# RWKV-6 attention and a SwiGLU block in one kernel: eps kept in a column of x, PSUM tiles that name their rings, and another written order

## The chip, the cores and the metric

One core of a Trainium2 chip runs the whole program. The metric is the device time of one execution in microseconds, the median of several runs.

## The reference

Two layers. The first is a linear-attention recurrence over 768 positions for 4 batches and 8 heads of 48 channels; the second normalises its output and puts it through a gated feed-forward block.

```python
state = np.zeros((B, H, D, D))                       # B, H, S, D = 4, 8, 768, 48
for t in range(S):
    cur = einsum('bhd,bhe->bhde', u * k[t], v[t])
    y[t] = einsum('bhd,bhde->bhe', r[t], state + cur)
    state = w[t][..., None] * state + einsum('bhd,bhe->bhde', k[t], v[t])
x = y.transpose(0, 2, 1, 3).reshape(B * S, H * D)    # 3072 x 384
xn = x / sqrt(mean(x * x) + 1e-6) * rms_g
g = xn @ w_gate                                      # 384 x 1536
out = (g * sigmoid(g) * (xn @ w_val)) @ w_out        # 1536 x 384
```

## The kernel before, in words

The sequence is cut into six blocks of 128 positions, numbered n from 0 to 5; j is the batch (0 to 3) and a block of all four batches has 512 tokens. Blocks 0 and 1 are loaded together (256 positions, one load for each of r, k, v, w and each batch) and handled as a pair. Within a block the recurrence is written as matmuls. `ln` takes the logarithm of w (ACT), `cs_mm` and `cs_k` sum it along the positions (PE), `exp_r` and `exp_k` turn the sums into decay factors (ACT), `r_mul` (DVE) and `k_mul` (POOL, some on DVE) apply them to r and k. `rk_pe` transposes the result on PE for blocks 0 and 1, with `rk_tr` as the copy out of PSUM; for later blocks `rk_tr` is a transposing DMA. `q_mm` makes the scores, `q_mask_e` (DVE) masks the even heads, `q_copy_o` copies the odd heads out (ACT, or masked on DVE where `ODD_DVE` says so), and `q_mask_o` (POOL) masks them where ACT only copied. The diagonal term goes over `bonus_mul` (two POOL instructions), `bonus_sum` (DVE) and `bonus_v` (POOL). `cast_v` puts v into bf16, `st_mm` and `st_new` carry the state on, `y_mm` makes the output of the attention.

Then comes the norm: `x_add` (DVE) adds the diagonal term, `x_sq` squares and sums (ACT), `x_rstd` takes the power -1/2 (two POOL instructions, or ACT), `xn_mul` scales, `xn_pe` and `xn_out` transpose and apply the gain (blocks 4 and 5: a transposing DMA, `xn_tr`, and `xn_gain`). In the feed-forward part a block has 12 units `gate_mm`, `silu`, `val_mm`, `h_mul` of six 256-column matmuls in block 0 and three 512-column matmuls later, and then one `o_mm`, `o_out`, `out_dma` for each batch; the last batch of block 5 is cut into three of these (j = 3, 4, 5: 192, 96 and 96 columns).

Block 0's gates and vals begin once `xn_out.0.0` and `xn_out.1.0` are done. Their weights come in two groups, units 0 to 3 and 4 to 11, by `load_gv.g.h` (g the group; h = 0 for gate, 1 for val), and `w_out` in three by `load_wo`; these loads convert to bf16 and are issued by POOL, in its queue. All other loads and the stores are issued by SP.

The order of the work is written out by hand: the string `ORDER` lists steps `function.n.j`, the program emits them in that order, and each engine carries out its own instructions in the order in which they were emitted. `warm` is a matmul on zeros whose result nobody reads.

PSUM has eight banks in three rings, a (2), b (2) and q (4). `psum` gives a step the bank whose last reader stands furthest back. Gates use a, vals b, everything small q, cumulative sums a and b.

```python
slots = rings[ring]
k = min((x for x in range(len(slots)) if slots[x][0] < at[0]), key=lambda x: slots[x])
...
slots[k] = [last_use.get(key, -1), taken[0]]
return psP.tile(shape, dtype, name="ps_" + ring + "uvxz"[k])
```

In the profile a bank is named by ring and letter: `ps_au`, `ps_bv`, `ps_qz`. Line 646 holds the matmuls of gates and vals, 683 those of o_mm, 238 all ACT functions with a table, 248 and 258 the loads of r, k, v, w, 350 and 353 the loads of weights, 464 and 465 bonus_mul, 457 k_mul, 475 bonus_v, 536 q_mask_o, 589 and 590 x_rstd on POOL.

## Time and profile before

| What | Value |
|---|---|
| Time, median of 3 runs | 199.3 us (199.29 to 199.4) |
| Span of the profiled execution | 197.6 us (its own device time is not listed; the runs' median is 1.7 us above this span) |
| PE (matmul) busy | 191.5 us, 97%, 1742 matmuls |
| PE weight loads busy | 120.4 us, 61% |
| DVE | 156.4 us, 79%, 315 instructions |
| ACT | 139.1 us, 70%, 286 |
| POOL | 127.5 us, 64%, 181 |
| Granted TensorE clock | 1.0 throughout |
| DMA | 32.42 MB, 155 GB/s of HBM traffic over the span |

A busy share is time in which the engine carried out something. PE's matmuls overlap each other in the records, so its share alone does not say that it had no slack; the waits and the chain do. A row of the timeline gives start, duration, engine, line, operation, output and inputs, and in brackets how long the engine had been idle and what ended that. "To landing" of a DMA counts from its issue.

### The profile page before, as it was taken

How to read it: one execution, taken by the hardware profiler on the slowest of the kernel's cores; microseconds unless marked ns; L12 is line 12 of the kernel's file. 1: busy time of each engine (PE TensorE's matmuls, PEld its weight loads, DVE VectorE, ACT ScalarE, POOL GpSimd, SP SyncE). 2: the span in 40 equal slices, each digit the busy share in tenths (PEclk: the TensorE clock that was granted, in tenths of full speed). 3: DMA queues.
4: the chain of work that ended last, by engine and by line, in shares of the span. 5: the costliest groups of instructions: out<-in, count | busy, mean ns of one | idle time of the engine just before them, and what ended most of it. 6: DMA issues, size and time to landing. Idle time of an engine off the chain costs nothing.

```text
span 197.6 us, 4751 instructions
## 1 busy us (share of the span) xinstructions
PE 191.5 (97%) x1742; PEld 120.4 (61%) x1742; DVE 156.4 (79%) x315; ACT 139.1 (70%) x286; POOL 127.5 (64%) x181
## 2 busy tenths in 40 slices
...
GB/s 164 320 325 267 244 220 205 220 213 197 174 230 162 199 179 214 200 211 214 185 206 225 202 147 166 227 51 145 134 216 12 5 60 60 20 63 80 40 60 101
DMA packets 109807, 32.42 MB, mean 164 GB/s; under 512 B 104276, under 2 KB 108632, under 8 KB 109784
## 3 DMA queue, kind: packets, MB, share of 16 engines
...
q10 hardware_dynamic: 8, 0.00, 0.0%
HBM read 25.96 MB, written 4.72 MB: 155 GB/s over the span
## 4 chain that ended last, share of the span: by engine, by line
PE 83%; DMA 7%; POOL 6%; SPq 1%; issue 1%; ACT 0%; POOLq 0%
PE ps_bu L646 13%; PE ps_bv L646 12%; PE ps_av L646 11%; PE ps_au L646 11%; PE ps_qv L683 7%; PE ps_qx L683 6%; PE ps_qz L683 6%; DMA wv_sb<-in_moe_w_val_dram 5%; PE ps_qu L683 5%; DMA kt<-in_k_dram 2%; POOL ruk L464 1%; POOL ruk L465 1%; SPq L248 1%; POOL qts L536 1%; PE ps_qz L513 1%
## 5 line engine op out<-in xcount | busy, mean ns | idle before, releaser
L238 ACT ACTIVATE sg<-ps_av 128x512 bf16<-128x512 f32 x36 | 21.5, 596 | 27.1 <-PE ps_av L646 21.4
L683 PEld LDWEIGHTS <-ht 128*128 128x128 bf16 x312 | 28.6, 98 | 18.3 <-DVE ht L666 0.4
L646 PEld LDWEIGHTS <-wg_sb 128*128 128x128 bf16 x252 | 27.0, 114 | 16.6 <-issue 0.3
L646 PEld LDWEIGHTS <-wv_sb 128*128 128x128 bf16 x252 | 26.4, 114 | 16.0 <-DMA wv_sb<-in_moe_w_val_dram 0.7
L666 DVE TENSOR_TENSOR ht<-ps_bu,sg 128x512 bf16<-128x512 f32 x37 | 25.4, 687 | 10.7 <-PE ps_bu L646 8.3
L666 DVE TENSOR_TENSOR ht<-ps_bv,sg 128x512 bf16<-128x512 f32 x35 | 24.0, 686 | 9.9 <-PE ps_bv L646 8.5
L646 PE MATMUL ps_bu<-xnt,wv_sb 128*128 128x512 bf16 (+1 forms) x135 | 30.3, 343 | 0.5 <-DMA wv_sb<-in_moe_w_val_dram 0.5
L646 PE MATMUL ps_av<-xnt,wg_sb 128*128 128x512 bf16 (+1 forms) x126 | 29.4, 350 | 0.0
L646 PE MATMUL ps_au<-xnt,wg_sb 128*128 128x512 bf16 (+1 forms) x126 | 29.3, 349 | 0.1
L646 PE MATMUL ps_bv<-xnt,wv_sb 128*128 128x512 bf16 (+1 forms) x117 | 28.5, 358 | 0.0
L464 POOL TENSOR_TENSOR ruk<-rt,kt 128x384 f32<-128x384 f32 x24 | 24.0, 1002 | 1.9 <-DVE diag L469 1.4
L465 POOL TENSOR_TENSOR ruk<-ruk,u_bc 128x384 f32<-128x384 f32 x24 | 24.0, 1000 | 1.9
L238 ACT ACTIVATE sg<-ps_au 128x512 bf16<-128x512 f32 x36 | 21.5, 596 | 4.5 <-PE ps_au L646 3.3
L457 POOL TENSOR_TENSOR rk<-kt,ek 128x384 bf16<-128x384 f32 x20 | 19.8, 1001 | 6.6 <-DMA kt<-in_k_dram 5.5
L475 POOL TENSOR_TENSOR ydiag<-vt,diag 128x384 f32<-128x384 f32 x24 | 19.9, 836 | 1.0 <-DVE diag L469 1.0
L236 ACT ACT_TABLE_LOAD x14 | 18.0, 1283 | 1.9 <-PEq L729 1.6
L536 POOL TENSOR_SCALAR_AFFINE_SELECT qts<-qts 128x512 bf16<-128x512 bf16 x19 | 11.9, 637 | 11.2 <-ACT qts L533 8.0
L683 PE MATMUL ps_qv<-wo_sb,ht 128*128 128x384 bf16 (+1 forms) x96 | 15.5, 311 | 0.0
L581 ACT ACTIVATE junk<-xb 128x384 bf16<-128x384 f32 x24 | 12.5, 521 | 4.2 <-DVE xb L576 3.9
L469 DVE TENSOR_REDUCE diag<-ruk 128x8 f32<-128x384 f32 x24 | 13.0, 544 | 0.0
L683 PE MATMUL ps_qx<-wo_sb,ht 128*128 128x384 bf16 x72 | 12.7, 326 | 0.0
L683 PE MATMUL ps_qz<-wo_sb,ht 128*128 128x384 bf16 x72 | 12.7, 326 | 0.0
(212 smaller groups left out, 376.8 us busy)
## 6 DMA issues: line engine op xcount, KB each, us to landing
...
wt<-in_w_dram SPq DMA_DIRECT2D x4, 384.0 KB, 4.3
rt<-in_r_dram SPq DMA_DIRECT2D x4, 384.0 KB, 4.9
kt<-in_k_dram SPq DMA_DIRECT2D x4, 384.0 KB, 4.9
```

Of the source, the lines that this page charges most:

```text
L236: nc.scalar.preload_act_table_set(table_name)
L238: return nc.scalar.activation(**kw).ins
L457: eng.tensor_tensor(out=rk[:, n % 2, j, 1, :, 0:D], in0=inp["k", n, j], in1=bank["cs_k", n, j][:, 0:DM].rearrange("p (h d) -> p h d", h=H) ...
L464: eng.tensor_tensor(out=ruk[n, j], in0=inp["r", n, j], in1=inp["k", n, j], op=ALU.mult)
L465: eng.tensor_tensor(out=ruk[n, j], in0=ruk[n, j], in1=u_bc, op=ALU.mult)
L469: nc.vector.tensor_reduce(out=diag[n, j].rearrange("p h o -> p (h o)"), in_=ruk[n, j], axis=mybir.AxisListType.X, op=ALU.add)
L475: eng.tensor_tensor(out=ydiag[n, j], in0=inp["v", n, j], in1=diag[n, j].to_broadcast([128, H, D]), op=ALU.mult)
L536: nc.gpsimd.affine_select(out=qts[n, j][:, 1], in_=qts[n, j][:, 1], compare_op=ALU.is_ge if n < 2 and j // 4 < n else ALU.is_gt, fill=0.0, ...
L581: nc.scalar.activation(out=junk, in_=xb[n, j], func=AF.Square, accum_out=rstd[n, j][:, 0:1])
L646: nc.tensor.matmul(ps.rearrange("p (i t) -> p i t", t=cols.stop - cols.start)[:, i, :], lhsT=units(ws, c, fs.start + i), rhs=xnt[n][:, c, ...
L666: nc.vector.tensor_tensor(out=ht[n][:, fs, cols], in0=bank.pop(("v", n, f)).rearrange("p (i t) -> p i t", i=fs.stop - fs.start), in1=bank. ...
L683: nc.tensor.matmul(ps[:, cols], lhsT=ht[n][:, f, b * L:(b + 1) * L], rhs=wo_sb[:, f, cols], start=(f == 0), stop=(f == FC - 1))
```

## The change

Four things, all in one edit.

- `ORDER` is another order of nearly the same steps. Steps for `warm` go from 34 to 41, those for `q_mask_o` from 19 to 18; all other steps are the same ones in other places.
- The sets that choose an engine for a step change: which `cast_v`, `xn_mul`, `rk_tr`, `q_copy_o`, `x_rstd`, `o_out` run on ACT, DVE or POOL. By count, DVE gets five more xn_mul and one more q_copy_o, and gives up one rk_tr and four o_out (two of them of part width) to ACT; POOL gets two more casts and gives up one mask.
- `MOVED_Q`, `MOVED_A`, `MOVED_B` name PSUM tiles that take their bank from another ring than their function's.
- x lives in four slots of one tile `xrow`, each with a 385th column that holds sqrt(eps x 384), set once. `x_sq` squares 385 columns with a scale of 384^-1/2, so its sum is already mean + eps; `x_rstd` needs one POOL instruction instead of two, and no `eps_col`.

```diff
 ORDER = """
 warm.200.0 warm.201.0 ... warm.209.0
-warm.210.0 warm.211.0 warm.212.0 load_w.0.0 load_w.0.1 ln.0.0 ln.0.1 load_r.0.0 load_k.0.0 cs_k.0.0 exp_k.1.0
-k_mul.1.0 cs_mm.0.0 exp_k.0.0 gu_mm.0.0 load_r.0.1 gu_out.0.0 load_k.0.1 exp_r.0.0 k_mul.0.0 bonus_mul.0.0 exp_r.1.0
-cs_mm.0.1 cs_k.0.1 exp_r.0.1 load_w.0.2 exp_k.0.1 r_mul.0.0 r_mul.1.0 load_w.0.3 r_mul.0.1 bonus_mul.0.1 bonus_mul.1.0
-exp_k.1.1 load_k.0.2 rk_pe.0.0 rk_tr.0.0 k_mul.1.1 rk_pe.1.0 warm.13.2 warm.14.2 warm.15.2 load_v.0.0 k_mul.0.1
-rk_tr.1.0 bonus_sum.0.0 w_tot.0.0 load_gv.1.0 exp_r.1.1 load_r.0.2 q_mm.0.0 warm.16.0 q_mm.1.4 warm.17.1 warm.18.2
-q_mask_e.0.0 r_mul.1.1 ln.0.2 ln.0.3 q_copy_o.0.0 cs_k.0.2 q_copy_o.1.4 exp_k.1.2 cs_mm.0.2 w_tot.0.1 q_mask_e.1.4
-bonus_v.0.0 load_v.0.1 q_mask_o.1.4 exp_k.0.2 q_mm.1.0 rk_pe.1.1 warm.19.1 warm.20.1 warm.21.2 q_copy_o.1.0
-bonus_sum.0.1 q_mask_e.1.0 exp_r.0.2 k_mul.1.2 cast_v.0.0 q_mm.0.4 warm.22.0 load_r.0.3 bonus_sum.1.0 load_k.0.3
-exp_r.1.2 q_copy_o.0.4 cast_v.1.0 rk_pe.0.1 rk_tr.0.1 q_mask_o.1.0 cs_mm.0.3 q_mask_e.0.4 rk_tr.1.1 r_mul.1.2
-bonus_v.1.0 exp_k.0.3 exp_r.0.3 y_mm.0.0 warm.23.0 q_mm.0.5 warm.24.0 warm.25.2 x_add.0.0 q_copy_o.0.5 y_mm.1.0
-q_mask_o.0.5 cast_v.1.1 q_mask_e.0.5 cast_v.0.1 load_v.0.2 r_mul.0.2 x_sq.0.0 x_add.1.0 rk_pe.1.2 load_w.2.0
-load_w.2.1 rk_tr.1.2 q_mm.0.1 warm.26.0 warm.27.0 warm.28.0 warm.29.2 q_copy_o.0.1 q_mask_e.0.1 exp_r.1.3 load_gv.1.1
-q_mm.1.1 warm.30.2 x_rstd.0.0 st_mm.0.0 k_mul.0.2 w_tot.0.2 x_sq.1.0 q_mask_e.1.1 xn_mul.0.0 load_v.0.3 bonus_v.0.1
-x_rstd.1.0 y_mm.0.1 rk_pe.0.2 q_copy_o.1.1 load_w.2.3 w_tot.0.3 xn_pe.0.0 st_new.0.0 xn_mul.1.0 x_add.0.1 cs_k.0.3
-rk_tr.0.2 exp_k.1.3 xn_out.0.0 x_sq.0.1 bonus_mul.1.1 r_mul.0.3 xn_pe.1.0 warm.31.1 warm.32.2 xn_out.1.0 q_mm.1.5
-warm.33.1 gate_mm.0.2 silu.0.2 gate_mm.0.3 silu.0.3 q_mask_o.1.1 q_mask_e.1.5 x_rstd.0.1 bonus_sum.1.1 q_copy_o.1.5
-q_mm.1.2 r_mul.1.3 load_r.2.0 k_mul.1.3 bonus_v.1.1 bonus_mul.0.3 y_mm.1.1 xn_mul.0.1 x_add.1.1 gate_mm.0.5
-gate_mm.0.4 q_mm.1.6 q_mask_e.1.2 load_gv.0.0 k_mul.0.3 q_copy_o.1.2 q_mask_e.1.6 silu.0.5 load_gv.0.1 bonus_mul.1.2
-rk_pe.1.3 rk_tr.1.3 val_mm.0.3 xn_pe.0.1 xn_out.0.1 h_mul.0.3 q_copy_o.1.6 x_sq.1.1 val_mm.0.5 x_rstd.1.1 q_mm.1.7
...
-gate_mm.0.1 cast_v.0.3 load_wo.1.0 x_sq.1.2 q_mask_o.0.6 silu.0.0 bonus_v.0.2 y_mm.0.2 q_mm.1.3 q_mask_e.1.3 silu.0.1
...
-out_dma.4.2 out_dma.4.3 silu.5.6 h_mul.5.6 o_mm.4.1 h_mul.5.5 silu.5.9 o_out.4.1 val_mm.5.10 out_dma.4.1 val_mm.5.9
-h_mul.5.9 gate_mm.5.10 silu.5.10 h_mul.5.10 o_mm.5.2 o_mm.5.3 o_out.5.2 o_out.5.3 o_mm.5.0 out_dma.5.2 o_out.5.0
-o_mm.5.1 out_dma.5.3 o_out.5.1 o_mm.5.4 out_dma.5.0 out_dma.5.1 o_mm.5.5 o_out.5.4 out_dma.5.4 o_out.5.5 out_dma.5.5
+warm.210.0 warm.211.0 warm.212.0 load_w.0.1 ln.0.1 cs_mm.0.1 load_w.0.0 ln.0.0 exp_r.0.1 w_tot.0.1 warm.0.1 cs_mm.0.0
+exp_k.0.0 exp_r.1.0 gu_mm.0.0 gu_out.0.0 load_r.0.0 load_k.0.0 r_mul.1.0 load_r.0.1 r_mul.0.1 load_k.0.1 cs_k.0.0
+exp_k.1.0 k_mul.1.0 k_mul.0.0 exp_r.0.0 w_tot.0.0 warm.1.1 warm.2.1 warm.3.1 warm.4.1 warm.5.1 warm.6.1 warm.7.1
+warm.8.1 warm.9.1 warm.10.1 warm.11.1 rk_pe.1.0 r_mul.0.0 cs_k.0.1 rk_pe.0.0 exp_k.0.1 load_w.0.2 exp_r.1.1 r_mul.1.1
+bonus_mul.1.0 k_mul.0.1 exp_k.1.1 rk_tr.1.0 ln.0.2 rk_tr.0.0 warm.12.1 q_mm.1.4 q_mask_e.1.4 q_copy_o.1.4 load_v.0.0
+warm.13.1 q_mm.1.0 q_copy_o.1.0 k_mul.1.1 q_mask_e.1.0 bonus_sum.1.0 cast_v.0.0 cs_mm.0.2 exp_k.0.2 bonus_mul.0.0
+cs_k.0.2 exp_k.1.2 bonus_sum.0.0 exp_r.0.2 rk_pe.0.1 rk_tr.0.1 q_mask_o.1.4 cast_v.1.0 bonus_v.0.0 q_mm.0.0
+q_mask_e.0.0 w_tot.0.2 q_copy_o.0.0 warm.14.2 warm.15.2 warm.16.2 warm.17.2 q_mm.0.4 exp_r.1.2 load_w.0.3 q_copy_o.0.4
+ln.0.3 load_k.0.2 k_mul.1.2 st_mm.0.0 st_new.0.0 load_v.0.1 q_mask_e.0.4 q_mask_o.0.0 rk_pe.1.1 rk_tr.1.1 load_r.0.2
+warm.18.0 cs_mm.0.3 r_mul.0.2 bonus_mul.0.1 r_mul.1.2 q_mm.0.5 k_mul.0.2 y_mm.0.0 cast_v.1.1 x_add.0.0 exp_r.0.3
+w_tot.0.3 q_copy_o.0.5 load_r.0.3 load_gv.1.0 r_mul.0.3 bonus_sum.0.1 q_mm.0.1 q_mm.1.1 cast_v.0.1 warm.19.0 warm.20.0
+rk_pe.1.2 q_copy_o.0.1 x_sq.0.0 q_mask_e.0.5 exp_k.0.3 exp_r.1.3 st_mm.0.1 q_mask_o.1.0 rk_tr.1.2 x_rstd.0.0
+xn_mul.0.0 load_k.0.3 q_mask_e.0.1 q_mask_e.1.1 r_mul.1.3 bonus_v.1.0 load_v.0.2 load_w.2.1 q_mask_o.0.5 cs_k.0.3
+q_mask_o.0.1 q_copy_o.1.1 load_v.0.3 load_w.2.0 exp_k.1.3 cast_v.0.2 load_gv.1.1 warm.21.1 warm.23.0 warm.22.1
+y_mm.1.0 x_add.1.0 cast_v.1.2 x_sq.1.0 bonus_v.0.1 load_v.2.1 q_mm.1.5 warm.24.1 rk_pe.0.2 q_copy_o.1.5 rk_tr.0.2
+q_mask_e.1.5 xn_pe.0.0 xn_out.0.0 y_mm.0.1 x_rstd.1.0 x_add.0.1 warm.25.1 warm.26.1 q_mm.1.2 st_new.0.1 xn_mul.1.0
+xn_pe.1.0 xn_out.1.0 q_mask_e.1.2 x_sq.0.1 q_mm.1.6 warm.27.1 gate_mm.0.5 x_rstd.0.1 xn_mul.0.1 silu.0.5 gate_mm.0.3
+silu.0.3 k_mul.1.3 gate_mm.0.2 bonus_mul.1.1 load_w.2.3 bonus_sum.1.1 q_copy_o.1.2 load_k.2.1 silu.0.2 q_copy_o.1.6
+y_mm.1.1 bonus_mul.1.2 q_mm.0.6 rk_pe.1.3 bonus_v.1.1 gate_mm.0.4 x_add.1.1 x_sq.1.1 bonus_sum.1.2 xn_pe.0.1 k_mul.0.3
+rk_pe.0.3 load_gv.0.1 q_mask_e.1.6 load_w.2.2 rk_tr.1.3 val_mm.0.3 x_rstd.1.1 rk_tr.0.3 xn_mul.1.1 load_gv.0.0
+bonus_mul.0.3 load_r.2.0 xn_out.0.1 load_wo.2.0 q_mask_e.0.6 q_copy_o.0.6 load_r.2.1 val_mm.0.2 bonus_v.1.2 h_mul.0.3
+ln.2.1 load_wo.0.0 h_mul.0.2 q_mm.1.7 xn_pe.1.1 ln.2.0 xn_out.1.1 val_mm.0.5 val_mm.0.4 bonus_mul.0.2 q_copy_o.1.7
...
+load_w.3.0 val_mm.0.0 load_v.2.0 load_k.2.0 x_sq.0.2 q_mask_e.0.3 q_mask_o.1.3 load_wo.1.0 x_rstd.0.2 q_mask_e.0.7
...
+silu.5.10 val_mm.5.10 h_mul.5.7 silu.5.5 h_mul.5.5 h_mul.5.10 o_mm.5.0 o_out.5.0 out_dma.5.0 o_mm.5.2 o_out.5.2
+out_dma.5.2 o_mm.5.3 o_out.5.3 o_mm.5.5 o_mm.4.3 out_dma.5.3 o_mm.5.1 o_out.5.5 o_out.4.3 out_dma.5.5 out_dma.4.3
+o_mm.5.4 o_out.5.1 out_dma.5.1 o_out.5.4 out_dma.5.4
 """
+    MOVED_Q = "cs_k.2.0 cs_k.2.1 cs_k.2.2 ... g.0.11 g.0.2 g.0.4 ... v.0.1 v.0.10 v.0.11 ..."
+    MOVED_A = "cs_k.1.1 cs_k.3.0 ... o.1.0 o.1.1 ... qe.0.0 ... v.2.11 ... y.5.3"
+    MOVED_B = "cs_k.1.2 g.0.0 g.0.5 ... st.0.1 ... xt.0.0 ... y.4.3"
-    XN_DVE = sel("02 21 23 42 43 51")
+    XN_DVE = sel("01 03 21 23 32 33 41 42 43 50 51")
-    RSTD_ACT = sel("00 10 11 21 22 23 41 42")
+    RSTD_ACT = sel("01 13 23 40 41 42 43")
...
     def psum(ring, key, shape, dtype=FP32):
+        ring = moved.get(key, ring)
         slots = rings[ring]
...
-    eps_col = small.tile([128, 1], FP32)
-    nc.vector.memset(eps_col, eps)
...
+    xrow = const.tile([128, NXB, DM + 16], FP32)
+    nc.vector.memset(xrow[:, :, DM:DM + 1], (eps * DM) ** 0.5)
...
     def x_add(n, j):
-        xb[n, j] = pt.tile([128, DM], FP32, name="xb", bufs=NXB)
-        nc.vector.tensor_tensor(out=xb[n, j], in0=bank.pop(("y", n, j)),
+        k = min((x for x in range(NXB) if xslots[x][0] < at[0]), key=lambda x: xslots[x])
+        xslots[k] = [xlast[n, j], NXB + at[0]]
+        xb[n, j] = xrow[:, k, 0:DM + 1]
+        nc.vector.tensor_tensor(out=xb[n, j][:, 0:DM], in0=bank.pop(("y", n, j)),
...
-        nc.scalar.activation(out=junk, in_=xb[n, j], func=AF.Square, accum_out=rstd[n, j][:, 0:1])
+        nc.scalar.activation(out=junk[:, 0:DM + 1], in_=xb[n, j], func=AF.Square, scale=DM ** -0.5,
+                             accum_out=rstd[n, j][:, 0:1])
...
-            act(LN_EXP, out=ss, in_=ss, func=AF.Ln, scale=1.0 / DM, bias=eps_col)
+            act(LN_EXP, out=ss, in_=ss, func=AF.Ln)
...
-            nc.gpsimd.tensor_scalar(out=ss, in0=ss, scalar1=1.0 / DM, scalar2=eps, op0=ALU.mult, op1=ALU.add)
             nc.gpsimd.tensor_tensor(out=rstd[n, j][:, 1:2], in0=ss, in1=mhalf, op=ALU.pow)
```

193 lines of the change are left out of this document (100 added, 93 removed).

## Prediction

> **What bounds the kernel now.** I read the stretches first, cutting the span at the first gate, at the first val and after the last matmul. A row gives the length, then busy time (instructions) of PE, PEld, DVE, ACT, POOL, then granted clock, DMA share, GB/s.
>
> ```profile
> 0.00:25.70 25.70, 23.13 (x268) 13.82 (x268) 21.85 (x61) 21.03 (x42) 18.99 (x33) 1.00 1.05 265
> 25.70:30.80 5.10, 4.53 (x66) 3.79 (x65) 5.10 (x10) 5.05 (x10) 4.84 (x7) 1.00 1.12 212
> 30.80:194.80 164.00, 163.88 (x1410) 102.82 (x1410) 129.49 (x246) 112.89 (x236) 103.62 (x143) 1.00 0.69 148
> 194.80:197.70 2.90, 0.00 (x0) 0.00 (x0) 0.00 (x0) 0.18 (x1) 0.00 (x0) 1.00 0.32 105
> ```
>
> From 30.8 us to 194.8 us PE is busy for 163.88 of 164.00 us, while DVE has 34 us to spare, ACT 51, POOL 60. PE runs its steps in the written order, so in that stretch a new order cannot win more than crumbs; it can only add waits. What is open is the lead-in: how late the stretch begins, and how much useful PE work is done by then. So next I read the chain of waits at that border, and the wait list.
>
> ```profile
> 20.98 9.76 DMA wv_sb<-in_moe_w_val_dram
> 30.79 0.84 PE ps_bu L646 x6
> ...
> 32.79 0.55 PE ps_qv L482 x8
> ...
> 34.16 0.34 PE ps_qx L545 x8
> ...
> 48.41 1.95 PE ps_qv L683 x12
> ```
>
> ```profile
> PE ps_bu L646 <- DMA wv_sb<-in_moe_w_val_dram: 0.5, 1, 0.5
> ```
>
> The stretch begins when the big block of `wv` (units 4 to 11, load_gv.1.1) lands. That load is issued by POOL's queue, so POOL's order sets it. The timeline of POOL, in full from its first real work to that issue:
>
> ```profile
> 8.18 1.00 POOL L457 TENSOR_TENSOR rk<-kt,ek 128x384 bf16<-128x384 f32 x1 [5.53 <-DMA kt<-in_k_dram]
> 9.13 1.00 POOL L464 TENSOR_TENSOR ruk<-rt,kt 128x384 f32<-128x384 f32 x1
> ...
> 11.16 1.00 POOL L464 TENSOR_TENSOR ruk<-rt,kt 128x384 f32<-128x384 f32 x1
> ...
> 13.20 1.01 POOL L464 TENSOR_TENSOR ruk<-rt,kt 128x384 f32<-128x384 f32 x1
> ...
> 15.24 0.99 POOL L457 TENSOR_TENSOR rk<-kt,ek 128x384 bf16<-128x384 f32 x1
> 16.17 0.99 POOL L350 DMA_DIRECT2D wg_sb<-in_moe_w_gate_dram  x1
> 17.19 0.84 POOL L475 TENSOR_TENSOR ydiag<-vt,diag 128x384 f32<-128x384 f32 x1
> 17.98 1.23 POOL L536 TENSOR_SCALAR_AFFINE_SELECT qts<-qts 128x512 bf16<-128x512 bf16 x2
> 19.17 0.82 POOL L475 TENSOR_TENSOR ydiag<-vt,diag 128x384 f32<-128x384 f32 x1
> 19.96 0.62 POOL L536 TENSOR_SCALAR_AFFINE_SELECT qts<-qts 128x512 bf16<-128x512 bf16 x1
> 20.54 0.49 POOL L384 CAST vb<-vt 128x384 bf16<-128x384 f32 x1
> 20.98 0.81 POOL L350 DMA_DIRECT2D wv_sb<-in_moe_w_val_dram  x1
> ...
> 26.32 0.18 POOL L589 TENSOR_SCALAR rstd<-rstd 128x1 f32<-128x1 f32 x1
> 26.59 0.57 POOL L590 TENSOR_TENSOR rstd<-rstd,mhalf 128x1 f32<-128x1 f32 x1
> 27.14 0.82 POOL L475 TENSOR_TENSOR ydiag<-vt,diag 128x384 f32<-128x384 f32 x1
> ```
>
> POOL starts at 8.18 us, when k of batch 0 is in, and then does not pause. From start to start: k_mul 0.95, a bonus_mul (two instructions) 2.03, bonus_v 0.79, q_mask_o 0.59, a cast 0.44, the pow of x_rstd 0.55 and its first instruction 0.27, a weight issue up to 1.02 us. From issue to landing (last column):
>
> ```profile
> wo_sb<-in_moe_w_out_dram POOLq DMA_DIRECT2D x3, 384.0 KB, 7.1
> wg_sb<-in_moe_w_gate_dram POOLq DMA_DIRECT2D x1, 768.0 KB, 8.4
> wv_sb<-in_moe_w_val_dram POOLq DMA_DIRECT2D x1, 768.0 KB, 9.8
> ```
>
> So `wg` landed at 16.17 + 8.4 = 24.6, just ahead of the first gate, and `wv` at 30.74, 6.2 us after it: the second follows the first.
>
> **The change, part by part.** *POOL's queue ahead of the weights* carries the forecast. Before, eight instructions stand between the arrival of k and the issue of `wg`: two k_mul and three bonus_mul. After, thirteen: k_mul.0.0, bonus_mul.1.0, k_mul.0.1, bonus_mul.0.0, q_mask_o.1.4, cast_v.1.0, bonus_v.0.0, q_mask_o.0.0, bonus_mul.0.1, k_mul.0.2. That is 3 x 0.95 + 3 x 2.03 + 2 x 0.59 + 0.44 + 0.79 = 11.35, so `wg` is issued at 8.18 + 11.35 = 19.5 us, 3.4 us later, and lands at 19.5 + 8.4 = 27.9. Then come the issue (1.02), q_mask_o.1.0 (0.59), x_rstd.0.0 (0.55), bonus_v.1.0 (0.79) and two masks (1.18): `wv` is issued at 23.7, 2.7 us later. It lands at 23.7 + 9.8 = 33.5 by its own latency, or at 27.9 + 6.2 = 34.1 if it again follows `wg`. I take 33.8, and the first val (val_mm.0.3 in both orders) at 33.85 instead of 30.79: 3.06 us later. Bounds: q_mask_o.0.0 may have to wait for ACT's copy, which I bound by one step of ACT's queue, 0.7 us (34.8); from below, the landings could take no time from the path at all (next paragraph).
>
> A sentence on the skill: the Trainium skill, page "DMA: Bandwidth & Descriptors", section "Anatomy of one DMA — SWDGE (gpsimd) path", fits a DMA from GpSimd as about 2.0 us plus its bytes over 436 GB/s, which is an estimate of 3.8 us for 768 KB and would put both weights in by 27.5 us, with no wait for them, so that the first rival below would hold. The trace has 8.4 and 9.8 us in this place, more than twice that, while the DMA share stands at 1.05 to 1.12; the sum goes by the trace.
>
> *If the weights did not wait*, DVE and POOL would set the border. DVE is busy for all of the 5.10 us of the second stretch, and it has three more steps ahead of xn_out.1.0, which the first gate needs: one r_mul (0.46), one q_mask_e (0.60) and one st_new (as r_mul).
>
> ```profile
> 24.63 0.54 DVE L451 TENSOR_TENSOR rk<-rt,ps_av 128x384 bf16<-128x384 f32 x1
> 25.09 0.55 DVE L619 TENSOR_TENSOR xnt<-ps_qx,gT 128x384 bf16<-128x384 bf16 x1
> 25.56 0.68 DVE L523 TENSOR_TENSOR qts<-ps_qv,up 128x512 bf16<-128x512 f32 x1
> 26.16 0.54 DVE L469 TENSOR_REDUCE diag<-ruk 128x8 f32<-128x384 f32 x1
> ```
>
> So the first gate moves from 25.79 to about 27.3 us by DVE alone. Between first gate and first val PE had 30.79 - 0.49 - 25.79 = 4.5 us of work; it loses a q_mm and gains a rk_pe and an xn_pe, some 4.7, so the first val could not come before 32.0. POOL says much the same: its k_mul.0.3, on which the rk_pe ahead of that val hangs, ends at 23.7 + 1.02 + 2 x 0.79 + 0.55 + 2 x 2.03 + 0.95 = 31.9.
>
> *PE's work done by then.* Ahead of the first val the new order has one more each of q_mm, rk_pe, xn_pe and st_mm, which it need not do later.
>
> ```profile
> 25.37 0.34 PE L377 MATMUL ps_av<-zero 128*128 128x384 bf16 x1
> 25.79 0.82 PE L646 MATMUL ps_au<-xnt,wg_sb 128*128 128x256 bf16 x6
> ...
> 27.19 0.23 PE L501 MATMUL ps_qx<-rkT 48*128 48x128 bf16 x1
> ...
> 27.52 0.57 PE L562 MATMUL ps_qz<-vb,qts 128*128 128x48 bf16 x16
> ...
> 31.47 0.33 PE L612 MATMUL ps_qv<-ident,xn 128*128 128x128 bf16 x3
> 31.64 0.82 PE L646 MATMUL ps_bv<-xnt,wv_sb 128*128 128x256 bf16 x6
> ```
>
> That is 0.33 (27.19 to 27.52) + 0.55 (L482 in the chain) + 0.17 (31.47 to 31.64) + 0.34 (L545) = 1.39 us. The 34 warm matmuls become 41, all ahead of the first gate: at most 7 x 0.34 = 2.4 us, nothing while PE waits there for weights and DVE as above; without that cover the 32.0 above would grow by part of it.
>
> *The tail.* The last two o_mm are now 5.1 (384 columns) and 5.4 (96), both copied out by ACT; before, two 96-column ones followed 5.1.
>
> ```profile
> 193.72 0.48 ACT L692 COPY ob<-ps_qz 128x384 f32<-128x384 f32 x1 [6.24 <-PE ps_qz L683]
> ...
> 194.74 0.24 ACT L692 COPY ob<-ps_qu 128x96 f32<-128x96 f32 x1 [0.54 <-PE ps_qu L683]
> ```
>
> The wide piece's copy used to start 1.02 us ahead of the last one; now it is 0.51, half of the gap, as one of the two narrow o_mm is ahead. Its own landing then ends the program instead of the narrow one's. I take 0.2 us more (between 0 and 0.51).
>
> *eps in a column.* One instruction less for each x_rstd on POOL (0.27 us each), a square over 385 columns instead of 384, no eps_col memset: on POOL and ACT, which have 60 and 51 us free after 30.8. In the lead-in only x_rstd.0.0 stands ahead of a weight issue, and there it is in the sum at 0.55. Nothing more.
>
> *PSUM rings and engines.* A ring's name costs no instruction. Gates and vals may now sit in the four banks of q, and then wait for a q_copy_o or x_add instead of a silu or h_mul; the list of waits has none of PE on a bank after 30.8, so there is nothing to win and an unknown number of short waits to lose, 0 to 1 us; I take 0, as the written distances between a bank's last reader and its next writer look alike in both orders. The moves between DVE and ACT (five more xn_mul on DVE, two more whole o_out and one more rk_tr on ACT) lie in idle time there. SP's queue lets v of batch 0 and three other input loads pass ahead of the weights, which come later; it waits for nothing new at the start, and what it carries later (stores, transposes of rk and xn) is under PE's 164 us.
>
> **The sum.** 3.06 later, less 1.39 of work done, plus 0.2 at the tail: + 1.87. The profiled span of 197.6 becomes 199.5; the median of 199.3 is 1.7 above that span, and with the same 1.7 around it I come to 201.2 us.
>
> **The rivals.** *No wait for weights.* If the loads land some 2 us faster, because the input loads that came before them are already in, the first val comes at 32.0: 32.0 - 30.79 - 1.39 + 0.2 = 0.0, so 199.3 us. For it: DMA is shared, and fewer input loads are left. Against: SP's queue goes on with the next ones, and the share was over 1 throughout the lead-in. *Faster.* A q_mm has a gap of about 0.09 us on either side (26.44 plus six matmuls to 27.19, and 27.52 after it), and the new order puts several q_mm side by side or at other neighbours. If the weights do not wait and four such pairs of gaps go, it is 199.3 - 0.7 = 198.6; it decides only once the weights are in by 32.0. *A second late weight.* The last block of w_out (load_wo.1.0) now stands behind q_mask_o.1.3 on POOL, so behind a q_mm and an ACT copy. I estimate its issue at 44 and landing at 51.1, with its 7.1. The first o_mm starts at 48.41 + 3.06 - 0.5 = 51.0 and wants that block 0.65 us later: half a microsecond of cover. Late by 1 us it is 202.2, and with bank waits after 30.8 up to 203.
>
> **How the numbers follow.** The forecast (200.2 to 202.0) 0.5; the second late weight or bank waits on top (to 203.2) 0.2; no wait for weights 0.17; faster 0.13. The range is 198.8 to 203.0. About 0.2% (0.4 us) is what a measurement of this kernel can tell from no change: faster 0.15, same 0.14, slower 0.71.
>
> **What would show it.** The POOL issue of `wg` near 19.5 and of `wv` near 23.7; PE's wait on `wv` (or on `wg` at the first gate) grown to 1 to 3 us; first val near 33.8; afterwards PE as full as before for some 162.6 us. It is wrong if the weights land within 6 to 7 us of their issue, if POOL reaches `wg` well before 19 us, or if PE shows new waits on banks after the first val.

## The result, and the profile after

| | Before | After |
|---|---|---|
| Median | 199.3 us (199.1 to 199.4) | 204.96 us (204.19 to 205.07) |
| Ratio, with its 95% interval | | 1.0268 (1.0238 to 1.0298) |
| Span of the profiled execution | 197.62 us | 202.48 us |
| First rk_pe | 9.74 us | 13.05 us |
| Issue of the big blocks of `wg`, `wv` | 16.17, 20.98 | 22.28, 26.84 |
| First gate, first val | 25.79, 30.79 | 30.89, 36.32 |

The kernel became slower, as forecast, but by 5.66 us and not by 1.9. The profiled execution took 204.19 us, the lowest of the runs after and 0.77 below their median, so the spans below account for 4.86 us of the loss. Medians and ratios leave out single executions that took over 1.5% more than the fastest of the same kernel; where a value comes from such an execution, the text says so.

Both spans cut at the first val, before first and then after; columns as in the prediction:

```profile
0.00:30.79 30.79, 27.65 (x332) 17.60 (x333) 26.94 (x70) 26.07 (x51) 23.83 (x39) 1.00 1.06 256
30.79:197.62 166.83, 163.89 (x1410) 102.83 (x1410) 129.50 (x246) 113.07 (x236) 103.63 (x143) 1.00 0.68 147
```

```profile
0.00:36.32 36.32, 32.55 (x366) 20.34 (x366) 29.41 (x73) 26.93 (x51) 26.41 (x42) 1.00 1.05 249
36.32:202.48 166.16, 161.96 (x1368) 101.66 (x1383) 129.02 (x244) 110.11 (x231) 99.58 (x126) 1.00 0.66 141
```

All of this loss, and a little more, lies ahead of the first val: 5.53 us there, -0.67 behind it, together 4.86. (In the last row 1368 matmuls stand beside 1383 weight loads, so a few matmul records are missing; PE's work behind the first val is taken below from e11, which has 1385.) The chain of waits of the changed kernel no longer begins with POOL alone:

```profile
12.89 0.32 PE ps_av L390
13.21 0.45 PE ps_qz L497 x8
...
14.47 0.53 DVE rkT L504
...
16.22 0.60 DVE qts L538
16.82 0.93 DVE diag L484 x2
...
17.82 0.83 POOL ydiag L490
...
22.34 0.91 POOL wg_sb L358
...
26.84 9.43 DMA wv_sb<-in_moe_w_val_dram
...
36.32 0.74 PE ps_qz L659 x5
```

It ends at the landing of `wv`, as before, but it now comes to POOL out of PE, by way of the eleven warm matmuls (L390) that the new order puts ahead of the first rk_pe (L497). Their rows in the timelines of PE and ACT:

```profile
9.10 4.11 PE L390 MATMUL ps_av<-zero 128*128 128x384 bf16 x11
13.05 0.61 PE L497 MATMUL ps_qz<-ident,rk 128*128 128x128 bf16 x8
```

```profile
14.02 0.56 ACT L248 ACTIVATE ps_av<-ps_av,down 128x384 f32<-128x384 f32 x1 [2.75 <-PE ps_av L434]
15.23 0.59 ACT L546 ACTIVATE qts<-ps_bu 128x512 bf16<-128x512 f32 x1
```

All eleven write one bank, `ps_av`, and take 0.38 us each from start to start. PE reaches rk_pe 3.3 us later than before, ACT stands 2.75 us, and so POOL stands too, which has to mask what ACT copied:

```profile
8.58 0.99 POOL L472 TENSOR_TENSOR rk<-kt,ek 128x384 bf16<-128x384 f32 x1 [5.91 <-ACT ek L248]
...
15.89 0.64 POOL L551 TENSOR_SCALAR_AFFINE_SELECT qts<-qts 128x512 bf16<-128x512 bf16 x1 [1.30 <-ACT qts L546]
...
17.82 0.83 POOL L490 TENSOR_TENSOR ydiag<-vt,diag 128x384 f32<-128x384 f32 x1 [0.84 <-DVE diag L484]
...
22.28 0.97 POOL L358 DMA_DIRECT2D wg_sb<-in_moe_w_gate_dram  x1
...
24.34 0.57 POOL L607 TENSOR_TENSOR rstd<-rstd,mhalf 128x1 f32<-128x1 f32 x1 [0.43 <-ACT junk L598]
...
26.84 0.84 POOL L358 DMA_DIRECT2D wv_sb<-in_moe_w_val_dram  x1
```

POOL starts 0.40 us later than forecast (in the experiments below this first step comes at other times again, 8.04 us in e8, so small differences are best counted from it) and pauses 1.30 + 0.84 us ahead of `wg`: 2.54 of the 2.8 us by which its issue misses the forecast 19.5. From issue to landing, and the two matmuls that want the weights:

```profile
wg_sb<-in_moe_w_gate_dram POOLq DMA_DIRECT2D x1, 768.0 KB, 8.2
wv_sb<-in_moe_w_val_dram POOLq DMA_DIRECT2D x1, 768.0 KB, 9.4
```

```profile
30.89 0.82 PE L659 MATMUL ps_bu<-xnt,wg_sb 128*128 128x256 bf16 x6
36.32 0.85 PE L659 MATMUL ps_qz<-xnt,wv_sb 128*128 128x256 bf16 x6 [0.24 <-DMA wv_sb<-in_moe_w_val_dram]
```

PE waits only 0.24 us for `wv`, and not at all for `wg`, which lands at 22.28 + 8.2 = 30.5. What ends last ahead of the first gate is the second block of x, on ACT and then on DVE:

```profile
29.17 0.67 ACT L614 ACTIVATE xn<-xrow,rstd 128x384 bf16<-128x384 f32 x1
```

```profile
30.28 0.56 DVE L636 TENSOR_TENSOR xnt<-ps_bv,gT 128x384 bf16<-128x384 bf16 x1
```

That xn starts 5.69 us later than before (23.48). Both spans cut there, before first and then after, in the same columns:

```profile
0.00:23.48 23.48, 20.99 (x245) 12.53 (x246) 19.63 (x56) 18.81 (x39) 16.85 (x30) 1.00 1.04 261
```

```profile
0.00:29.17 29.17, 26.33 (x279) 15.19 (x279) 22.39 (x61) 21.04 (x39) 19.57 (x35) 1.00 1.04 260
```

ACT has 2.23 us more work ahead of it (21.04 instead of 18.81; the new order puts five casts of v there instead of three, and one copy of rk and one of scores more) and stands idle for 8.13 us instead of 4.67, of which 2.75 behind the warm block. What the profile cannot say is what each of these late things costs by itself. That is what the experiments are for.

### The profile page after: what moved, and what is told of

It is laid out like the page before. It is cut to its first block, busy times and chain, and to the rows that moved or that the text cites. A ratio compares the mean times of both kernels' runs of the same rounds, so it can differ in the third digit from the quotient of the medians.

```text
span 202.5 us, 4716 instructions
## 1 busy us (share of the span) xinstructions
PE 194.5 (96%) x1734; PEld 122.0 (60%) x1749; DVE 158.4 (78%) x316; ACT 137.0 (68%) x281; POOL 126.0 (62%) x167
## 4 chain that ended last, share of the span: by engine, by line
PE 79%; DMA 6%; POOL 6%; DVE 5%; issue 2%; ACT 0%; DVEq 0%; ACTq 0%; POOLq 0%
PE ps_qz L659 7%; PE ps_bu L659 6%; PE ps_qu L659 6%; PE ps_bv L659 6%; PE ps_qv L659 6%; PE ps_av L659 5%; PE ps_au L659 5%; PE ps_qx L659 5%; DMA wv_sb<-in_moe_w_val_dram 5%; PE ps_av L696 4%; PE ps_bu L696 3%; PE ps_qu L696 2%; PE ps_au L696 2%; PE ps_qv L696 2%; PE ps_qx L696 2%
## 5 line engine op out<-in xcount | busy, mean ns | idle before, releaser
L659 PEld LDWEIGHTS <-wg_sb 128*128 128x128 bf16 x252 | 27.2, 114 | 17.0 <-issue 0.5
L607 POOL TENSOR_TENSOR rstd<-rstd,mhalf 128x1 f32<-128x1 f32 x17 | 9.4, 561 | 14.3 <-ACT junk L598 14.3
L598 ACT ACTIVATE junk<-xrow 128x385 bf16<-128x385 f32 x24 | 12.7, 530 | 7.5 <-DVE xrow L593 7.4
L248 ACT ACTIVATE lw<-wt 128x384 bf16<-128x384 f32 (+1 forms) x20 | 11.4, 586 | 1.7 <-DMA wt<-in_w_dram 1.6
L696 PE MATMUL ps_av<-wo_sb,ht 128*128 128x384 bf16 (+1 forms) x72 | 11.5, 306 | 0.1
L659 PE MATMUL ps_av<-xnt,wg_sb 128*128 128x512 bf16 (+1 forms) x46 | 10.5, 338 | 0.1
L248 ACT ACTIVATE sg<-ps_av 128x512 bf16<-128x512 f32 x13 | 7.8, 598 | 3.5 <-PE ps_av L659 3.5
L659 PE MATMUL ps_qz<-xnt,wv_sb 128*128 128x512 bf16 (+1 forms) x42 | 9.5, 336 | 0.5 <-DMA wv_sb<-in_moe_w_val_dram 0.2
L659 PE MATMUL ps_qu<-xnt,wg_sb 128*128 128x512 bf16 (+1 forms) x44 | 9.7, 336 | 0.1
L679 DVE TENSOR_TENSOR ht<-ps_qz,sg 128x512 bf16<-128x512 f32 x12 | 8.2, 684 | 1.5 <-ACT sg L248 0.9
L659 PE MATMUL ps_bu<-xnt,wg_sb 128*128 128x512 bf16 (+1 forms) x38 | 8.9, 346 | 0.1
```

The costliest lines, as they stand in the source:

```text
L248: return nc.scalar.activation(**kw).ins
L598: nc.scalar.activation(out=junk[:, 0:DM + 1], in_=xb[n, j], func=AF.Square, scale=DM ** -0.5, accum_out=rstd[n, j][:, 0:1])
L659: nc.tensor.matmul(ps.rearrange("p (i t) -> p i t", t=cols.stop - cols.start)[:, i, :], lhsT=units(ws, c, fs.start + i), rhs=xnt[n][:, c, ...
L679: nc.vector.tensor_tensor(out=ht[n][:, fs, cols], in0=bank.pop(("v", n, f)).rearrange("p (i t) -> p i t", i=fs.stop - fs.start), in1=bank. ...
L696: nc.tensor.matmul(ps[:, cols], lhsT=ht[n][:, f, b * L:(b + 1) * L], rhs=wo_sb[:, f, cols], start=(f == 0), stop=(f == FC - 1))
```

## The experiments

Each ran with runs of the kernel before beside it (their median 199.4 to 199.7 us); ratios are to these, and a cost in us is a difference of medians.

### e1: the changed kernel without its eleven early warms

```diff
-... exp_r.0.0 w_tot.0.0 warm.1.1 warm.2.1 ... warm.11.1 rk_pe.1.0 r_mul.0.0 ...
+... exp_r.0.0 w_tot.0.0 rk_pe.1.0 r_mul.0.0 ...
```

> The changed kernel without warm.1 to warm.11, the eleven warm matmuls that PE carries out at 9.1 to 13.05 us, 0.38 us each, all on one PSUM bank, ahead of the first rk_pe. Theory (the warm block holds PE, and through rk_pe, the masks and POOL's queue also the weights): the first rk_pe starts at 10.8 to 11.3 us instead of 13.05, POOL's pauses of 1.30 us (before q_mask_o.1.4) and 0.84 us (before bonus_v.0.0) shrink to under 0.5 together, wg is issued near 20 us instead of 22.28, wv near 24.5 instead of 26.84, the first val starts near 33.9 instead of 36.32, and the time falls from 205.0 to about 202.6 us. Rival (the order of POOL's and ACT's own steps makes the pauses): wg is still issued at 22 us or later and the time stays within 0.4 us of 205.0.

Measured 204.84 us (202.91 to 205.65), ratio 1.0235 (1.0169 to 1.0300). The four runs are two pairs: 202.91 and 204.47 us with the clock granted at 1.0, 205.20 and 205.65 with 0.992. The profiled one is of the second kind. POOL's timeline, then PE's:

```profile
19.89 0.97 POOL L357 DMA_DIRECT2D wg_sb<-in_moe_w_gate_dram  x1
```

```profile
29.68 1.30 PE L658 MATMUL ps_bu<-xnt,wg_sb 128*128 128x256 bf16 x6 [1.22 <-DMA wg_sb<-in_moe_w_gate_dram]
```

`wg` is issued 2.4 us earlier, near where the prediction had put it (11.60 us behind POOL's first k_mul; forecast 11.35, changed kernel 13.70): POOL's pauses came from the warm block. But the load now takes 9.7 us instead of 8.2 and lands only 0.8 us earlier, PE waits 1.22 us for it, and the stretches (granted clock third from the end) show the clock at that place:

```profile
28.00:30.00 2.00, 0.78 (x12) 0.43 (x7) 2.00 (x4) 1.70 (x4) 1.92 (x3) 0.98 1.18 230
30.00:32.00 2.00, 2.00 (x11) 1.39 (x10) 2.00 (x4) 0.60 (x1) 1.86 (x3) 0.50 1.13 210
32.00:34.00 2.00, 2.00 (x30) 1.51 (x29) 0.01 (x1) 1.06 (x2) 1.45 (x2) 0.67 0.92 176
```

The clock is granted by half for 3.4 us from about 29.9, just behind the wait, and the first val comes at 35.89. The Trainium skill, page "TensorE: Matmul & The Clock Gate", section "What's actually happening", says that the gate passes half or all of the clock and goes by windows of about 3.4 us; the trace agrees in both (0.50, and 3.4 us).

### e2: the same warms on three rings in turn

```diff
-... warm.1.1 warm.2.1 warm.3.1 warm.4.1 ... rk_pe.1.0 ...
+... warm.1.1 warm.2.2 warm.3.0 warm.4.1 ... rk_pe.1.0 ...
```

> The changed kernel with the same eleven warm matmuls, taking their banks in turn from the rings a, b and q instead of all from a. Theory (they are slow because each writes the bank that the one before it has just written): they start 0.16 us apart instead of 0.38, the block takes 1.8 us instead of 4.1, the first rk_pe starts at 10.9 to 11.3 us, and the time is within 0.5 us of that without them, near 202.6. Rival (a warm matmul costs 0.38 us here whatever its bank, or it is the slow clock): still some 4 us, and the time stays at 205.0.

Three runs took 203.15, 203.70 and 204.44 us, ratio 1.0195 (1.0143 to 1.0247); the fourth, which is the profiled one, took 206.70. The block takes 2.2 us instead of 4.0 (first rk_pe at 10.86) and `wg` is issued at 20.09. In the profiled execution the gate still comes only at 30.95, after a wait of 2.3 us for `wg`, which needed 10.8 us, and the clock is at half for 3.4 us from 31.9. So there, as in e1, the time won by POOL is not kept; the three faster runs may have kept more of it, and have no profile.

### e3 and e4: the two weight loads far up

e3 moves them in the changed kernel (the diff shows only where they go to); e4 does so without the early warms.

```diff
-... bonus_mul.1.0 k_mul.0.1 exp_k.1.1 ...
+... bonus_mul.1.0 k_mul.0.1 load_gv.1.0 exp_k.1.1 ...
-... q_mask_o.1.4 cast_v.1.0 bonus_v.0.0 ...
+... q_mask_o.1.4 cast_v.1.0 load_gv.1.1 bonus_v.0.0 ...
```

> The changed kernel with load_gv.1.0 moved up to right behind k_mul.0.1 and load_gv.1.1 to right behind cast_v.1.0, warm block as it is. Prediction's mechanism alone (the place of the weights in POOL's queue sets the border): wg issued near 12.5 us and wv near 18, no wait on weights, first val 3 us earlier, near 33, time near 202. Theory (the warm block has delayed DVE, POOL and ACT as well, so that the first gate's own inputs are late): the first gate stays within 0.7 us of 30.9 because xn_out.1.0 ends there, the first val comes near 35.3 to 35.8 us, and the time falls by 0.5 to 1 us only, to about 204.2.

> The changed kernel without warm.1 to warm.11 and with both weight loads moved up as in e3_weights_early. Theory: both limits go; first gate near 28.3 us, first val near 32.8, time near 201.3 us, below either edit alone. Rival (weights and warm block are the same 2.5 us seen twice): no better than e1_no_warm within 0.4 us.

e3 took 210.45 us, ratio 1.0513 (1.0459 to 1.0566), e4 210.65 us, ratio 1.0542 (1.0499 to 1.0585). No theory had this. In e3 `wg` is issued at 12.21, and then the inputs are late:

```profile
PE ps_qz L516 <- DVE rk L466: 4.8, 1, 4.8
```

The loads of r for blocks 0 and 1 take a median of 9.2 us instead of 4.8, and two of them 13.7. The first gate comes at 36.66, in e4, where the same wait is 6.7 us, at 35.80. In e3 the clock is at half for 6.8 us on top, from about 26.5. Weights and inputs take from one another: more of the one early is less of the other. The Trainium skill, page "DMA: Bandwidth & Descriptors", section "Queues, rings and completion order", says that each DMA engine goes round the queues that have work, packet by packet; the trace agrees as far as the input loads stretch (9.2 us instead of 4.8) while a weight load runs; it does not show the packets.

### e5: the kernel before, with only the weight loads late

```diff
-... w_tot.0.0 load_gv.1.0 exp_r.1.1 ...
+... w_tot.0.0 exp_r.1.1 ...
-... q_mask_o.0.5 cast_v.1.1 ...
+... q_mask_o.0.5 load_gv.1.0 cast_v.1.1 ...
-... exp_r.1.3 load_gv.1.1 q_mm.1.1 ... load_v.0.3 bonus_v.0.1 ...
+... exp_r.1.3 q_mm.1.1 ... load_v.0.3 bonus_v.0.1 load_gv.1.1 ...
```

> The kernel before with nothing changed but the place of two issues in POOL's queue: load_gv.1.0 behind q_mask_o.0.5, load_gv.1.1 behind bonus_v.0.1. That is the prediction's mechanism alone, in the size that it forecast: wg issued near 19.5 us instead of 16.2, wv near 22.7 instead of 21.0. Theory (the first val follows the issue of wg by the 14.6 us that it takes before): wg lands near 28, wv near 34.1, first val near 34.1 instead of 30.8, time near 202.6 us; if PE's wait lets its clock fall to half for a while, as without the warm block, up to 204.5. Rival (input loads that now go first make the rest of the lead-in earlier and pay for it): within 0.5 us of before.

204.24 us (203.95 to 205.12), ratio 1.0247 (1.0215 to 1.0279). The loads' place is enough to cost 4.6 us with nothing else changed, and what PE waits for is `wg`, at the first gate:

```profile
20.35 0.99 POOL L350 DMA_DIRECT2D wg_sb<-in_moe_w_gate_dram  x1
```

```profile
29.05 1.47 PE L646 MATMUL ps_au<-xnt,wg_sb 128*128 128x256 bf16 x6 [3.51 <-DMA wg_sb<-in_moe_w_gate_dram]
```

```profile
26.00:28.00 2.00, 0.00 (x0) 0.00 (x0) 1.70 (x4) 1.11 (x1) 1.82 (x5) 0.79 1.14 218
...
32.00:34.00 2.00, 2.00 (x30) 1.50 (x25) 0.80 (x2) 0.94 (x2) 1.98 (x3) 0.50 1.19 255
```

Part of it is the wait of 3.51 us (25.54 to 29.05), and part the half clock, here for 6.8 us. It begins inside the wait, at about 27.2, and lasts until 34.0, so PE works under it for 4.9 us and loses some 2.5 us by that. The clock is below 1.0 (0.982 to 0.992) in all runs of e5.

### e6: the kernel before, with a warm block as long as the new one

```diff
-... load_k.0.2 rk_pe.0.0 rk_tr.0.0 ...
+... load_k.0.2 warm.301.0 warm.302.0 ... warm.324.0 rk_pe.0.0 rk_tr.0.0 ...
```

> The kernel before with 24 more warm matmuls ahead of the first rk_pe, on the ring q (three banks free there), some 3.9 us at 0.16 us each: as long as the warm block of the changed kernel holds PE, by another number of matmuls. Theory (what costs is the time that PE is held ahead of its first transposes): first rk_pe at 12.5 to 13 us instead of 9.74, DVE pauses of 2 us there, first gate near 28.5, first val near 33, time 201.5 to 202.5 us, though wg is still issued at 16.2 us. Rival (the lead-in waits for weights anyway, so the hold is hidden): wg and wv issued as before, first val within 0.7 us of 30.8, time within 0.5 us of before.

202.21 us (202.08 to 202.53), ratio 1.0143 (1.0116 to 1.0170): the block alone is worth 2.6 us there. `wg` keeps its 16.14, and behind it POOL waits for the mask's input:

```profile
23.06 0.63 POOL L539 TENSOR_SCALAR_AFFINE_SELECT qts<-qts 128x512 bf16<-128x512 bf16 x1 [2.50 <-ACT qts L534]
...
24.09 0.81 POOL L353 DMA_DIRECT2D wv_sb<-in_moe_w_val_dram  x1
```

`wv` is 3.1 us later at the issue and lands after 8.1 us, at 32.2; the first val comes at 33.27, 2.5 us late. PE waits for neither weight: `wg` is in at 24.0, the first gate comes at 28.92, 3.1 us late, and the first val follows it. So the block's cost reaches the gate and the val through the engines that PE feeds; `wv`, in 1.1 us ahead of the val, is not what it waits for.

### e7: the kernel before, with only eps in a column

```diff
+    xrow = const.tile([128, NXB, DM + 16], FP32)
+    nc.vector.memset(xrow[:, :, DM:DM + 1], (eps * DM) ** 0.5)
...
-            nc.gpsimd.tensor_scalar(out=ss, in0=ss, scalar1=1.0 / DM, scalar2=eps, op0=ALU.mult, op1=ALU.add)
```

> The kernel before with the eps column alone: x in slots of one tile, the square over 385 columns, one POOL instruction less for each x_rstd; order, engines and rings as before. Prediction: no change that can be measured, within 0.4 us of before. Rival (the shared tile xrow ties the slots together and adds waits, or a wider square delays ACT): 0.5 us or more slower.

199.26 us (eight runs; two more took 202.4 and 202.9), ratio 0.9979 (0.9954 to 1.0005): no change that can be told, as costed.

### e8: the early warms away, seven others at the first gate

```diff
-... w_tot.0.0 warm.1.1 ... warm.11.1 rk_pe.1.0 ...
+... w_tot.0.0 rk_pe.1.0 ...
-... xn_mul.1.0 xn_pe.1.0 ... warm.27.1 gate_mm.0.5 ...
+... xn_mul.1.0 warm.1.1 warm.2.1 xn_pe.1.0 ... warm.27.1 warm.3.1 ... warm.7.1 gate_mm.0.5 ...
```

> The changed kernel without the early block of eleven warm matmuls, but with two of them put ahead of xn_pe.1.0 and five ahead of the first gate, where PE waits for weights. Theory (the early block costs 2 us through POOL's queue, and without it some runs lose the gain again because PE idles ahead of the first gate and its clock is granted at half for 3.4 us): wg issued near 20 us as without the block, clock 1.0 throughout, first gate near 29.8, first val near 34.3, time 202.5 to 203 us in all its runs. Rival (the clock falls for another reason, or DMA sets it all): a spread of 203 to 205.7 as without the block.

203.57 us (203.11 to 203.94), ratio 1.0205 (1.0177 to 1.0232), the clock full in all runs. So the early block costs about 1.4 us in the changed order, where seven other warms stand ahead of the first gate. `wg` is issued at 19.64 (forecast 19.5) and lands after 10.0 us, at 29.6. First gate 30.08, first val 34.60. This is the nearest that the runs come to the prediction's own picture, POOL without pauses and the clock at full, and it still takes 2.4 us more than the 201.2 forecast.

### e10 and e11: the weights back at the times of the kernel before

e11 makes this move in the changed kernel, e10 in e8 (the diff shows only where the loads go to).

```diff
-... cast_v.1.0 bonus_v.0.0 q_mm.0.0 ...
+... cast_v.1.0 bonus_v.0.0 load_gv.1.0 q_mm.0.0 ...
-... q_mm.0.5 k_mul.0.2 y_mm.0.0 ...
+... q_mm.0.5 k_mul.0.2 load_gv.1.1 y_mm.0.0 ...
```

> The changed order without its eleven early warms, seven warms at the first gate, and the two 768 KB weight loads moved back to where the kernel before has them in time: wg's issue right behind bonus_v.0.0 (by the POOL rows of e8: 16.1 us, before 16.17), wv's right behind k_mul.0.2 (20.6 us, before 20.98). Theory (the weights' place is what is left): with the 8.4 and 9.8 us of the kernel before, wg lands at 24.5 and wv at 30.4, the first val matmul comes near 31 instead of 34.60, and the time near 203.6 - 3.6 = 200.0. Rival (the input loads are as short as in e3): PE waits for rk or xn instead, the first val comes at 33 or later and the time is 202 to 206, with a row of 1 us or more at PE for DVE or POOL.

> The changed kernel with its early warms, only the two weight loads moved up, behind bonus_v.0.0 and k_mul.0.2. By its own POOL rows wg is issued at 18.7 instead of 22.28 and wv at 23.3 instead of 26.84. Theory (the weights' place and the warm block add up): first val near 33 instead of 36.3, time near 205 - 3.3 = 201.7. Rival (the input loads push back as in e3): 204 or more, PE waiting for an operand made of the inputs.

e10 took 206.01 us in the profiled run and 211 to 213.1 us in three others. In the profile the clock is at half from about 11 to 18 us, so from before the first moved load is issued (16.21). The same steps have a full clock there in e8; why not here is open, and nothing is read from e10 about the weights.

e11 took 205.1 us (204.34 to 205.51), ratio 1.0264 (1.0218 to 1.0310): as slow as the changed kernel, although `wg` is issued at 18.11 and lands after 8.5 us, at 26.6, and `wv` is in at 33.1. The theory in which the costs of warm block and weights simply add up is wrong. ACT's timeline of e11, then PE's:

```profile
28.68 0.68 ACT L614 ACTIVATE xn<-xrow,rstd 128x384 bf16<-128x384 f32 x1
```

```profile
30.41 0.81 PE L659 MATMUL ps_bu<-xnt,wg_sb 128*128 128x256 bf16 x6
...
35.51 0.81 PE L659 MATMUL ps_qz<-xnt,wv_sb 128*128 128x256 bf16 x6
```

The first gate needs the x of two batches, and the second xn starts on ACT at 28.68 (changed kernel: 29.17; before: 23.48). The gate follows 1.7 us behind it, in both. POOL's first k_mul stands at 8.09 in e11 and at 8.58 in the changed kernel; counted from it, second xn (20.59 us) and gate (22.3 us) are where they were. So a weight that landed 4 us earlier moved the gate by nothing: in the changed kernel the second xn held it, and `wg`, at 30.5, came just ahead. The first val gained 0.3 us, about what PE had waited for `wv`.

### e13, e14, e15: the third limit

e13 is e11 with the warms on three rings as in e2. e14 is e13, and e15 the changed kernel, with two casts of v moved on ACT from ahead of the second xn to behind the third gate:

```diff
-... exp_k.1.3 cast_v.0.2 load_gv.1.1 ... x_add.1.0 cast_v.1.2 x_sq.1.0 ...
+... exp_k.1.3 load_gv.1.1 ... x_add.1.0 x_sq.1.0 ...
-... silu.0.3 k_mul.1.3 gate_mm.0.2 bonus_mul.1.1 ...
+... silu.0.3 k_mul.1.3 gate_mm.0.2 cast_v.0.2 cast_v.1.2 bonus_mul.1.1 ...
```

(In e13 and e14 load_gv.1.1 stands further up.)

> The changed kernel with both of its two late things taken away: the eleven early warms on three rings in turn (the block is then 2.2 us shorter, as in e2) and the two weight loads behind bonus_v.0.0 and k_mul.0.2 (wg issued at 16.5 us and wv at 21 by the POOL rows of e2). Theory (two limits of nearly the same time: the landing of wg, and the second xn on ACT that the warm block pushed to 29.17; e2 and e11 each took one away and gained little): the second xn comes near 27.0 as in e2, the first gate near 28.4, the first val near 33.4 by the 5.1 us between them in e11, and the time near 202.2, or 203.9 where the clock is granted by half for 3.4 us as in e2's profile. Rival (the changed order of ACT itself, not the block, holds the first gate back): first gate at 30 or later although wg has landed, and 204.5 or more at full clock.

e13 took 208.73 us (208.16 to 209.97), ratio 1.0469 (1.0427 to 1.0511). The theory missed; its rival, which laid the late gate on ACT's own order, comes nearer, though it did not name the place. ACT's timeline and PE's:

```profile
30.52 0.92 ACT L395 CAST vb<-vt 128x384 bf16<-128x384 f32 x2 [5.55 <-DMA vt<-in_v_dram]
```

```profile
32.92 0.29 PE L516 MATMUL ps_qu<-rkT 48*128 48x128 bf16 x1 [5.88 <-ACT rkT L506]
```

ACT stands 5.55 us at a cast of v. The load was issued at 17.37, just behind `wg` (16.49), and took 13.13 us; in e11 the same load was issued at 16.36, ahead of `wg` (18.11), took 7.5 us, and ACT does not wait for it. The changed order has five casts on ACT ahead of the first gate where the one before had three, so it needs more of the input in before the gate; weights that were issued early pushed just that back here.

> e13 with the two casts cast_v.0.2 and cast_v.1.2 moved on ACT from ahead of the second xn to behind the third block of gate matmuls. Theory (three limits meet at the first gate: the landing of the weights, the warm block, and an input load of vt that the changed order needs before the gate): ACT's 5.55 us wait for vt is gone from there, the second xn comes at 26 to 27, the first gate at 28 to 28.5, the first val near 33.4, and the time falls by some 5 us, from 208.7 to 202 to 204. Rival (the wait goes to the next user of a late input load, on DVE, POOL or PE): another wait of 3 us or more for rk, xrow or a load, and 207 or more.

> The changed kernel with only these two casts moved. Theory: the second xn comes 1 us earlier on ACT (28.2 instead of 29.17), but wg still lands near 30.5 and wv near 36.3, so the first gate and the first val stay, and the time stays within 0.6 of 205.0. Rival (ACT's queue alone holds the gate): first gate at 29.9 and 204.0 or less.

e14 took 203.23 us (202.19 to 203.51), ratio 1.0178 (1.0145 to 1.0211): 5.5 us less than e13 for two casts in another place, a part of it the half clock of e13, which begins inside the wait and lasts from about 29.6 to 36.5. In e14 the same load of v takes 13.0 us again, but no cast stands at it ahead of the gate. ACT and PE of e14:

```profile
26.82 0.61 ACT L614 ACTIVATE xn<-xrow,rstd 128x384 bf16<-128x384 f32 x1
```

```profile
28.48 0.82 PE L659 MATMUL ps_bu<-xnt,wg_sb 128*128 128x256 bf16 x6
...
33.64 0.82 PE L659 MATMUL ps_qz<-xnt,wv_sb 128*128 128x256 bf16 x6
```

e15 took 205.14 us (204.47 to 206.91), ratio 1.0300 (1.0239 to 1.0361): no gain by the same two casts where the other limits stand. Its second xn starts at 28.61, and its gate at 30.27, with `wg` landing at 21.79 + 8.3 = 30.1. That gate lies between the two numbers expected, and both limits end within 0.2 us of each other; the time is the one of the theory. ACT's timeline shows why the xn is hardly earlier, counted from POOL's first k_mul: without the casts ACT waits instead, for DVE's x_add.

```profile
27.18 0.53 ACT L598 ACTIVATE junk<-xrow 128x385 bf16<-128x385 f32 x1 [0.58 <-DVE xrow L593]
```

### e12: the kernel before with eps in a column, and `wv` one instruction earlier

```diff
-... q_mask_o.0.5 cast_v.1.1 q_mask_e.0.5 cast_v.0.1 ... exp_r.1.3 load_gv.1.1 q_mm.1.1 ...
+... q_mask_o.0.5 load_gv.1.1 cast_v.1.1 q_mask_e.0.5 cast_v.0.1 ... exp_r.1.3 q_mm.1.1 ...
```

> The kernel before with the eps column, and wv's first load one POOL instruction earlier (ahead of the 0.49 us cast of vt that precedes it). If the landing of wv sets the start of the full stretch, as the chain says, the first val comes up to 0.5 us earlier and the time is 0.2 to 0.5 us lower (198.9 to 199.2). Rival (wv's bytes wait for those of wg, whose issue is unchanged): no change, 199.3 to 199.5.

198.96 us (eleven runs; a twelfth took 203.3), ratio 0.9974 (0.9946 to 1.0002). `wv` is issued at 20.41 instead of 20.98, lands after 10.1 us instead of 9.8, and the first val comes at 30.55 instead of 30.79:

```profile
30.55 0.85 PE L651 MATMUL ps_bu<-xnt,wv_sb 128*128 128x256 bf16 x6 [0.35 <-DMA wv_sb<-in_moe_w_val_dram]
```

The direction fits the theory, but the interval touches 1. So no version here is shown to beat the kernel before.

## Why the prediction was right and wrong

**Right.** The direction was right, and so was the place: all of the loss lies ahead of the first val, and behind it PE is as full as before, without new waits on banks and without a second late weight. The mechanism, weights that POOL's queue issues later, is shown by itself in the kernel before (e5), at the first gate and with the half clock on top. In the changed kernel it is one of two limits, and not the one that ends last: the sign that the prediction named for it, a wait of PE of 1 to 3 us for a weight, did not come (0.24 us). The rival without a wait for weights falls as it was argued: it needed landings some 2 us faster, and the traces here give 7.9 to 10.8 us for 768 KB. The Trainium skill, page "DMA: Bandwidth & Descriptors", section "Anatomy of one DMA — SWDGE (gpsimd) path", has a fit from which the prediction worked out an estimate of 3.8 us; no trace here agrees with it. eps in a column brings no change that can be told (e7), and the tail grew by 0.07 us (forecast 0.2): from the last matmul's start to the end 3.19 instead of 3.12.

**Luck.** The latencies of the sum (8.4 and 9.8) look as if they had held (8.2 and 9.4), but these are the latencies of an issue that came 2.8 us later than forecast. Where POOL issues `wg` near the forecast 19.5, the load takes 9.7 us (e1) and 10.0 us (e8), and lands at 29.6 instead of the forecast 27.9.

**The first step that failed** is the issue of `wg` at 8.18 + 11.35 = 19.5 us. It takes over from the trace of before that POOL "then does not pause", with 0.7 us as the bound for one mask, while the 41 warms were counted ("at most 7 x 0.34 = 2.4 us, nothing while PE waits there") and not placed. Eleven of them stand ahead of the first rk_pe, long before PE waits for anything, all on one bank at 0.38 us each, so that they hold PE for 4.0 us. What PE feeds comes later by that: ACT stands 2.75 us, POOL pauses 1.30 and 0.84 us, and `wg` is issued at 22.28 (e1, without the block: 19.89). In e6 such a block alone costs 2.6 us, in the changed order (against e8) 1.4.

**The second step that failed** is the larger one: the floor without weights. "If the weights did not wait", the first gate was put at about 27.3 us by DVE alone, and the first val at 32.0. ACT was not asked. With the weights in at 26.6 and 33.1 (e11), the gate came at 30.41 and the first val at 35.51, 3.5 us above that floor, held by ACT's second xn; with the block short as well (e13), by the load of v that ACT's casts wait for; and with these casts out of the way too (e14) the gate came at 28.48. So two things end within half a microsecond of each other ahead of the first gate, and a third stands behind them, which comes up as soon as `wg` is issued ahead of that load of v. Taking away one brings little (e2 1.3 us and e8 1.4; e1, e11 and e15 nothing that can be told), taking away two a loss (e13), and all three 1.7 us (e14), which is not shown to be more than e2 or e8. That ACT's second xn is late is read from the profile; which of ACT's added steps make it so was tested only for the two casts.

**Mis-sized terms.** The first val is 5.53 us later, and the prediction had 3.06. PE's work done by then was put at 1.39 us; e11, which has the same steps behind the first val and nearly all matmul records, has 163.03 us busy in its stretch against 163.89 before, so it is 0.86. What is left of 166.16, 3.13 us, is PE without work there, against 2.94; the tail's 0.07 is part of that. The sum is 5.53 - 0.86 + 0.19 = 4.86 us of span. The bank waits, taken as 0 of 0 to 1, are within those 0.19. The PSUM rings alone were not tried, so their own price is not shown.

**What stays open.** e14 is still 3.7 us slower than the kernel before, so most of the loss is not given a cause by an experiment. Its second xn starts at 26.82, still 3.34 us later than before, its first val is 2.85 us later, and its stretch after that is longer, not shorter:

```profile
33.64:201.70 168.06, 162.20 (x1371) 101.54 (x1383) 130.09 (x244) 110.37 (x231) 99.65 (x126) 1.00 0.67 142
```

That is 1.9 us more than in the changed kernel for the same steps, 1.3 of it in one wait of PE that e11 has too:

```profile
PE ps_au L659 <- POOL xnt L641: 1.3, 1, 1.3
```

So an earlier start is partly given back later, and which of the moved steps hold the changed order's lead-in at 33.6 even then was not taken apart.
